# A timed pause on GpSimd in place of a limit on gathers in flight, in a kernel that sums a long convolution and a table of experts

## The chip, the cores and the metric

The kernel runs on one core of one Trainium2 chip. The metric is the device time of one execution in microseconds. Three runs of the kernel before took 960.07, 968.80 and 969.19 us; their median is 968.8 us.

## The reference

Input is `x`, 2048 rows of 448 numbers, and its row-wise layernorm `xn`. The output is `x` plus two branches that both read `xn`:

```
A: k_shift = causal depthwise convolution of k with 4 taps
   kv      = k_shift * v
   y       = causal convolution of kv with ssm_k (2048 taps, per channel, by FFT) + kv * ssm_D
   A       = xn * y
B: q       = xn @ w_q                      16 heads, two halves of 256
   s1, s2  = the halves against 64 keys each; the top 2 of each, the best 2 of the 4 sums
   e       = 64 * i1 + i2                  2 experts of 4096 per head: 32 per row
   out     = sum over the 32 of softmax(score) * gelu(xn . u[e]) * v[e]
```

Branch B reads 32 rows of `u` and 32 of `v` for each of 2048 rows, 3584 bytes a pair. That is 512 gathers of 128 pairs.

## The kernel before

Everything is float32. The 2048 rows are 16 tiles `T` of 128 partitions. `u` and `v` stand side by side in one DRAM table `uv`, so that one indexed row brings both.

*Weights* (`w_*`): `w_q` is multiplied by the keys once, which gives a matrix 448 x 2048 that maps `xn` to all scores; it is kept as a high and a low part.

*Scores* (`s_*`), tile by tile: `s_turn` transposes `xn`, `s_split` makes high and low parts, `s_mm` (L348 to L360) does the matmuls, `s_top` (L379 to L400) finds the best 8 of each 64 on VectorE (DVE) with `max` and `max_index`, and `s_gate`, `s_place` and `s_put` write for each tile the expert numbers `idx` and the gate weights `gt`.

*Experts* (`e_*`): the 32 experts of a tile's rows are laid out so that one gather brings, for 32 rows, 4 experts each onto 128 partitions. Four gathers fill one buffer `uv` (128 x 4 x 896 numbers); this document calls them a burst. There are 128 bursts and four buffers (`NBUF`). For each burst:

- `e_gather` (L490): four indirect DMAs issued by GpSimd (POOL). The first of them needs the buffer free, that is, the value matmuls of the burst four places earlier done.
- `e_dots` (L522): `xr`, the rows of `xn` spread over partitions by a matmul (`e_spread`, L503), times the gathered `u`. DVE multiplies `na` of the four in one instruction (L531), and ScalarE (ACT) sums those (`e_gelu`, L545); the other 4 - `na` DVE multiplies and sums by itself (L538). In the scores stage `na` is 4, later it is chosen by the planner's loads of the two engines.
- gelu on ACT, the gate weight on DVE (L565), and `cc`, the weights as a matmul operand, by DVE (L570) or ACT (L580).
- `e_values` (L583): the gathered `v` weighted and added on TensorE (PE), into `pv` (L593). This frees the buffer.
- after two bursts `e_out` copies `pv` (L603); after eight, `e_fold` sums on PE (L612) and DVE adds to the output rows `acc` (L614).

*Convolution* (`c_*`): the 448 channels are 112 groups of 4, and two halves `g` of 56 groups go one after the other. In each half there are an input stage (`c_load` brings `hkv` by SP in seven loads; `c_tap` and `c_prod` form `kv`; `c_in` on PE and `c_store` on ACT do the first step of the transform), a spectral stage over 33 frequencies (`c_fm` loads one matrix for each; `c_spec` L711, `c_hh`, `c_mul` with four DVE instructions L728 to L734, `c_inv` L743, `c_turn` L751), and an output stage (`c_back`, `c_zt`, `c_fin` L779, `c_gate` L788 and L793). Scores and convolution share memory, so the convolution begins behind the last score. `e_store` (L616) stores a tile's channel half by SP once that tile's experts are folded and the half's last gate is done.

*What sets the order.* The instructions of each engine run in the order in which the program emits them. That order comes from a planner (L97 to L182) that runs when the kernel is built: each operation is an `Op` with an engine, a planned cost in microseconds, and keys it waits for; the planner keeps a clock per engine, takes the operation that can start first, and settles near ties by priority. A gather has a planned cost of 1.25 on POOL, and a planned landing by its bytes. `need` (L824) makes scores urgent when they are less than `LEAD` gathers ahead of POOL's planned work. `turn` (L839) keeps the convolution in step with the gathers: it compares the share of the convolution's planned work that is done with the share of POOL's planned work since the scores' end, up to 640.0, which is 512 times 1.25. The planner sets the order only; at run time semaphores hold each instruction until its data are there.

*The limit.* `e_gather` keeps a list `sent` of all gathers and adds to each one a dependence on the gather four places earlier (L500), so a gather is issued only when that one has landed.

Of the kernel before, what the change touches and what calls it, by code (L numbers as in the profile page):

```python
# [185 lines left out]
def parallel_kernel(ctx, tc, x, wq, kk, uv, hkv, const, fq, out):  # L186
    nc = tc.nc
    ctx.enter_context(tc.manual_schedule())
    ap = ctx.enter_context(tc.tile_pool(name="ap", bufs=1))
# [8 lines left out]
    plan = Planner()  # L198
    r_sc, r_xr, r_a, r_v, r_uv = Ring(3), Ring(1), Ring(2), Ring(1), Ring(NBUF)
# [5 lines left out]
    rep = ap.tile([P, 4, 32], F32, name="rep")  # L205
    fold = rep[:, 0, :]
    half = ap.tile([P, 1], F32, name="half")
    mv = ap.tile([P, NT, 2], F32, name="mv")
    rstd = ap.tile([P, NT], F32, name="rstd")
    nmr = ap.tile([P, NT], F32, name="nmr")  # L210
    idx = ap.tile([P, NT, NG], I32, name="idx")
# [14 lines left out]
    live = {}  # L226
# [106 lines left out]
    def s_turn(tiles):  # L333

        for T in tiles:
            def turn(T=T):
                live["px", T] = ps_sc.tile([P, 512], F32, tag="sc", name="px")
                for c in range(KC + 1):
                    n = P if c < KC else KR
                    nc.tensor.matmul(live["px", T][:n, P * c:P * c + P], xn[:, T, P * c:P * c + n], ident, start=(c == 0), stop=False, skip_group_check=True)  # L340
            yield Op("PE", 0.75, turn, [("xn", T)] + ([("sc", T - 2, 3)] if T > 1 else []), key=("px", T), rings=[(r_sc, ("xl", T))], lag=0.2)
            def less(T=T):
                px, xh = live["px", T], live["xh", T][0]
                nc.tensor.matmul(px[:, :P * KC], minus, xh[:, :KC].rearrange("p c n -> p (c n)"), start=False, stop=True, skip_group_check=True)
                nc.tensor.matmul(px[:KR, P * KC:], minus[:KR, :KR], xh[:KR, KC], start=False, stop=True, skip_group_check=True)
            yield Op("PE", 0.6, less, [("xh", T)], key=("pl", T), lag=0.2)
# [138 lines left out]
    NB = len(order)  # L485
    HALF = CH * GC

    sent = []

    def e_gather():  # L490
        for b, (T, j, hf) in enumerate(order):
            for c in range(4):
                def go(b=b, T=T, g=8 * j + 4 * hf + c, c=c):
                    if c == 0:
                        live["uv", b] = gp.tile([P, 4, 2 * D], F32, tag="uv", name="uv")
                    made = nc.gpsimd.indirect_dma_start(live["uv", b][:, c, :], None, uv, bass.IndirectOffsetOnAxis(ap=idx[:, T, g:g + 1], axis=0)).ins  # L496

                    sent.append(made)
                    if len(sent) > 4:
                        tc.add_manual_dep(made, sent[-5].name, mybir.DependencyInfo(mybir.DependencyClass.Sync, mybir.DependencyReason.DATA), reason="pace")  # L500
                yield Op("POOL", 1.25, go, [("idx", T)], key=("land", b, c), moved=4.6e5, rings=[(r_uv, ("v", b))] if c == 0 else [])

    def e_spread():  # L503
        for T in range(NT):
# [299 lines left out]
    rest = range(2, NT)  # L804
# [9 lines left out]
    plan.add(2, norm(6, NT))  # L814
    plan.show("weights")
    experts = [plan.add(PRIO.get(s.__name__, 0.0), s()) for s in (e_gather, e_values, e_weigh, e_scale, e_spread, e_dots, e_gelu, e_out, e_fold)]
    stores = [plan.add(1, e_store(g)) for g in range(2)]
    plan.run(early)
# [18 lines left out]
    begun = plan.busy["POOL"]  # L837

    def turn():  # L839
        e = (plan.busy["POOL"] - begun) / (640.0 - begun)  # L840
        return -1 if plan.spent.get("conv", 0.0) / WORK < e + AHEAD else 1
    conv = []
    for g in range(2):
        for i, s in enumerate((c_load(g), c_delta(g), c_in(g, 0), c_store(g, 0), c_tap(g), c_prod(g), c_in(g, 1), c_store(g, 1),
                  c_fm(g), c_spec(g), c_hh(g), c_mul(g), c_inv(g), c_turn(g), c_back(g), c_zt(g), c_fin(g), c_gate(g))):
            conv.append(plan.add(lambda p=PRIO.get(s.__name__, 0.0): turn() + p, s, "conv"))
# [44 lines left out]
```

## Time and profile before

| | |
|---|---|
| median of three runs | 968.8 us |
| the profiled execution's own time | 975.48 us |
| its span, first to last instruction | 973.7 us |
| PE, DVE, ACT, POOL busy | 738.4, 711.1, 544.8, 492.0 us |
| mean granted clock of TensorE | 0.861 |
| moved by DMA | 278.52 MB, of it 234.91 MB by gathers |

The page lists for each engine its busy time, and for each group of instructions (line, engine, operation, what it writes and reads) how often it ran, its busy time and mean duration, the idle time of its engine just before it, and what ended that idle time. The chain is the work that ended last, followed back. DMA share is the mean busy share of the 16 DMA engines. PE rows are partly modelled, and a row on POOL is rough.

### The profile page before, as it was taken

The numbers are of one execution on the slowest core, as the hardware profiler recorded it, in microseconds if no ns is written. First come the engines' busy times: TensorE is split into PE (matmuls) and PEld (weight loads), VectorE is DVE, ScalarE is ACT, GpSimd is POOL, SyncE is SP. The second block draws the span as 40 slices with busy tenths as digits, with TensorE's granted clock in tenths as the row PEclk, the third lists the DMA queues.
The fourth block names the chain that finished last, engine by engine and source line by source line (L and its number), as shares of the span: only waits on it lengthen the run. The fifth ranks groups of instructions, "written<-read, shape, count | busy, mean of one in ns | idle before, by whom it ended". The sixth has DMA issues, their size and how long they took to land.

```text
span 973.7 us, 16544 instructions
## 1 busy us (share of the span) xinstructions
PE 738.4 (76%) x5052; PEld 421.8 (43%) x5052; DVE 711.1 (73%) x2621; ACT 544.8 (56%) x1886; POOL 492.0 (51%) x518
## 2 busy tenths in 40 slices
PE   6982989798987878846567787777777668786765
PEld 3561545455554545414344343334544424343443
DVE  3587978888787978765487788875586769788433
ACT  4325875566665665665375565554375555565532
POOL 0025562556655655555465465654545655556440
PEclk9995899898989978866677799988877898899877
DMA  9938784889888878899987699999978879999764
GB/s 344 381 125 297 248 311 152 277 280 314 292 281 275 295 263 285 271 307 377 316 284 253 219 337 330 337 310 371 319 258 264 307 266 324 327 312 338 237 219 140
DMA packets 80553, 278.52 MB, mean 286 GB/s; under 512 B 10320, under 2 KB 47568, under 8 KB 80464
## 3 DMA queue, kind: packets, MB, share of 16 engines
q0 software_dynamic: 40960, 234.91, 69.9%
q1 hardware_dynamic: 39360, 42.41, 13.0%
q8 instruction: 41, 0.67, 0.3%
q14 instruction: 48, 0.39, 0.1%
q10 hardware_dynamic: 144, 0.13, 0.1%
HBM read 273.75 MB, written 3.67 MB: 285 GB/s over the span
## 4 chain that ended last, share of the span: by engine, by line
PE 26%; DVE 23%; DMA 13%; issue 11%; ACT 9%; another core or an unknown queue 6%; POOL 5%; SPq 1%; DVEq 0%; POOLq 0%; ACTq 0%
DMA uv<-in_uv_dram,idx 11%; DVE uv L531 9%; ACT uv L550 5%; PE pv L593 5%; POOL uv L496 5%; DVE mi L397 4%; PE fin L779 3%; PE ps L683 3%; DVE mx L399 3%; DMA x<-in_hkv_dram 2%; PE sc L355 2%; PE sc L356 2%; PE sc L357 2%; PE psf L711 1%
## 5 line engine op out<-in xcount | busy, mean ns | idle before, releaser
L496 POOL DMA_INDIRECT uv<-in_uv_dram,idx x512 | 491.3, 960 | 458.4 <-issue 125.9
L550 ACT ACTIVATE uv<-uv 128x448 f32<-128x448 f32 x459 | 258.7, 567 | 80.0 <-DVE uv L531 52.5
L531 DVE TENSOR_TENSOR uv<-xr,uv 128x1792 f32<-128x1792 f32 (+3 forms) x128 | 233.2, 1823 | 38.2 <-DMA uv<-in_uv_dram,idx 21.6
L593 PE MATMUL pv<-uv,cc 128*32 128x448 f32 x1024 | 160.8, 652 | 0.2 <-ACT uv L550 0.2
L397 DVE FIND_INDEX8 mi<-mx,sc 128x8 uint32<-128x64 f32 x512 | 104.3, 221 | 7.4 <-issue 7.3
L683 PE MATMUL ps<-cst,x 128*64 128x132 f32 x896 | 82.2, 341 | 34.0 <-ACT x L693 23.3
L683 PEld LDWEIGHTS ps<-cst,x 128*64 128x64 f32 x896 | 65.6, 171 | 70.8 <-ACT x L693 38.8
L711 PE MATMUL psf<-x,fm 128*128 128x448 f32 x132 | 71.3, 630 | 30.9 <-DVE hh L734 10.1
L399 DVE MAX8 mx<-sc 128x8 f32<-128x64 f32 x512 | 73.7, 213 | 24.2 <-remote 11.5
L355 PE MATMUL sc<-wh,xh 128*128 128x512 f32 x192 | 85.3, 444 | 5.5 <-DVE mx L399 2.3
L550 ACT ACTIVATION_READ_ACCUMULATOR uv<-uv 128x1 f32 x459 | 87.2, 190 | 0.0
L356 PE MATMUL sc<-wl,xh 128*128 128x512 f32 x192 | 79.3, 413 | 0.6 <-issue 0.6
L357 PE MATMUL sc<-wh,xl 128*128 128x512 f32 x192 | 78.4, 409 | 0.3 <-issue 0.3
L743 PE MATMUL psu<-hh,fm 128*128 128x224 f32 x264 | 67.6, 386 | 9.7 <-ACT x L751 5.7
L590 PE MATMUL pv<-uv,cc 128*1 128x4 bf16 x128 | 21.6, 169 | 68.9 <-DVE cc L570 24.8
L743 PEld LDWEIGHTS psu<-hh,fm 128*128 128x128 f32 x264 | 52.7, 207 | 40.7 <-issue 27.3
L693 ACT ACTIVATE x<-ps 128x396 f32<-128x396 f32 (+1 forms) x84 | 37.2, 459 | 51.0 <-PE ps L683 34.4
L590 PEld LDWEIGHTS <-cc 128*1 128x1 bf16 x128 | 10.3, 80 | 122.3 <-issue 40.4
L565 DVE TENSOR_TENSOR w<-ge,gt 128x4 f32<-128x4 f32 x128 | 19.9, 156 | 57.1 <-ACT ge L554 41.4
L779 PE MATMUL fin<-cst,zt 128*64 128x64 f32 x896 | 46.7, 258 | 19.4 <-issue 18.8
L580 ACT ACTIVATE cc<-rep,w 128x32 f32<-128x32 f32 x212 | 50.1, 311 | 14.4 <-DVE w L565 6.1
L355 PEld LDWEIGHTS sc<-wh,xh 128*128 128x128 f32 x192 | 38.7, 201 | 42.0 <-issue 18.5
(98 smaller groups left out, 1063.0 us busy)
## 6 DMA issues: line engine op xcount, KB each, us to landing
wq<-in_wq_dram SPq DMA_DIRECT2D x16, 896.0 KB
x<-in_hkv_dram SPq DMA_DIRECT2D x14, 780.0 KB
fm<-in_fq_dram SPq DMA_DIRECT2D x66, 128.0 KB
uv<-in_uv_dram,idx POOLq DMA_INDIRECT x512
out_dram<-acc SPq DMA_DIRECT2D x32, 112.0 KB
acc<-in_x_dram SPq DMA_DIRECT2D x1, 2240.0 KB
acc<-in_x_dram SPq DMA_DIRECT2D x1, 896.0 KB
cst<-in_const_dram SPq DMA_DIRECT2D x1, 540.0 KB
```

The source lines that it names most:

```text
L355: nc.tensor.matmul(sc, xh[:, c, :], wh[:, c, ns], start=(c == 0), stop=False)
L356: nc.tensor.matmul(sc, xh[:, c, :], wl[:, c, ns], start=False, stop=False)
L357: nc.tensor.matmul(sc, xl[:, c, :], wh[:, c, ns], start=False, stop=False)
L397: nc.vector.max_index(mi[:, T % 2, 8 * n + j, :], m, sc[:, 64 * j:64 * j + 64])
L399: nc.vector.max(m, sc[:, 64 * j:64 * j + 64])
L496: made = nc.gpsimd.indirect_dma_start(live["uv", b][:, c, :], None, uv, bass.IndirectOffsetOnAxis(ap=idx[:, T, g:g + 1], axis=0)).ins
L531: nc.vector.tensor_mul(u, live["xr", T, j][:, None, :D].broadcast_to([P, na, D]), u)
L550: nc.scalar.activation(u, u, AF.Copy, accum_out=live["act", b][:, c:c + 1])
L593: nc.tensor.matmul(pv[32 * c:32 * c + 32, :D], cc[:, c, :], buf[:, c, D:], start=(hf == 0), stop=(hf == 1), tile_position=(0, 32 * c))
L683: nc.tensor.matmul(ps[64 * i:64 * i + 64, w * j:w * j + w], src, f1[:, i, :], start=True, stop=True, tile_position=(0, 64 * i))
L711: nc.tensor.matmul(ps[:, :2 * HALF], live["fm", g, q][:, 0], x1[:, :, :, q, :].rearrange("p c t k -> p t c k"), start=True, stop=True)
L743: nc.tensor.matmul(ps[:, :HALF], fm[:, 1], hh[:, i], start=(i == 0), stop=(i == 1))
```

## The change

The list `sent` and the dependence on the gather four places earlier go. Behind each fourth gather, the last of a burst, POOL runs a `memset` of 512 bytes in one partition of a new tile `idle` that nothing reads. The planner is told: the fourth gather's cost is 2.10 instead of 1.25, which makes 5.85 for a burst, and `turn` counts POOL's work up to 749.0, which is 128 times 5.85.

```diff
+    idle = ap.tile([1, 512], mybir.dt.uint8, name="idle")
...
-    sent = []
-
     def e_gather():
         for b, (T, j, hf) in enumerate(order):
             for c in range(4):
                 def go(b=b, T=T, g=8 * j + 4 * hf + c, c=c):
                     if c == 0:
                         live["uv", b] = gp.tile([P, 4, 2 * D], F32, tag="uv", name="uv")
-                    made = nc.gpsimd.indirect_dma_start(live["uv", b][:, c, :], None, uv, bass.IndirectOffsetOnAxis(ap=idx[:, T, g:g + 1], axis=0)).ins
-
-                    sent.append(made)
-                    if len(sent) > 4:
-                        tc.add_manual_dep(made, sent[-5].name, mybir.DependencyInfo(mybir.DependencyClass.Sync, mybir.DependencyReason.DATA), reason="pace")
-                yield Op("POOL", 1.25, go, [("idx", T)], key=("land", b, c), moved=4.6e5, rings=[(r_uv, ("v", b))] if c == 0 else [])
+                    nc.gpsimd.indirect_dma_start(live["uv", b][:, c, :], None, uv, bass.IndirectOffsetOnAxis(ap=idx[:, T, g:g + 1], axis=0))
+                def rest(go=go):
+                    go()
+                    nc.gpsimd.memset(idle, 0)
+                yield Op("POOL", 1.25 if c < 3 else 2.10, rest if c == 3 else go, [("idx", T)], key=("land", b, c), moved=4.6e5, rings=[(r_uv, ("v", b))] if c == 0 else [])
...
-        e = (plan.busy["POOL"] - begun) / (640.0 - begun)
+        e = (plan.busy["POOL"] - begun) / (749.0 - begun)
```

Each of the two programs has the same gathers, matmuls and transfers. What else differs follows from the plan: the order on every engine, and how many dot products go by which of the two ways (DVE alone does 62 instead of 53, ACT sums 450 instead of 459; DVE makes `cc` 80 times instead of 75).

## The prediction

> **What bounds the kernel now.** I read the page first: busy times, queues, then the costliest groups.
>
> ```profile
> span 973.7 us, 16544 instructions
> ...
> PE 738.4 (76%) x5052; PEld 421.8 (43%) x5052; DVE 711.1 (73%) x2621; ACT 544.8 (56%) x1886; POOL 492.0 (51%) x518
> ...
> q0 software_dynamic: 40960, 234.91, 69.9%
> ...
> L496 POOL DMA_INDIRECT uv<-in_uv_dram,idx x512 | 491.3, 960 | 458.4 <-issue 125.9
> ```
>
> No engine is full. The gathers' queue q0 holds the 16 DMA engines for 69.9% of the span, which is 680.6 us for 512 gathers, or 1.33 us each. POOL takes 0.96 us per gather and is otherwise idle, so something makes it wait. An average can't say what, so I cut the span by the kernel's stages: scores with experts, the two spectral stages (L711 to L751, once per channel half), and the end.
>
> ```profile
> core 0: us, PE busy (x) PEld busy (x) DVE busy (x) ACT busy (x) POOL busy (x), PEclk, DMA share, GB/s
> 162.00:426.00 264.00, 221.85 (x1206) 131.61 (x1204) 217.85 (x1250) 165.59 (x630) 154.75 (x164) 0.91 0.85 283
> 545.00:651.00 106.00, 84.15 (x392) 41.26 (x384) 91.28 (x188) 62.92 (x219) 64.00 (x68) 0.95 0.92 324
> 794.00:897.00 103.00, 78.87 (x360) 39.33 (x360) 86.90 (x175) 59.01 (x204) 60.88 (x65) 0.92 0.93 325
> 897.00:974.00 77.00, 49.13 (x617) 32.12 (x617) 33.82 (x68) 29.30 (x87) 26.07 (x28) 0.82 0.60 205
> ```
>
> In the scores window PE (84%) and DVE (83%) are both nearly full. In the spectral windows DVE stands at 86% and 84% and the DMA share at 0.92 and 0.93. Next, POOL's gathers in the scores window (first row), the first spectral window (second and third) and the second one (fourth), with what ended its idle time, and its two longest waits at the end (last two).
>
> ```profile
> L496 POOL DMA_INDIRECT uv<-in_uv_dram,idx x164 | 155.0, 945 | 122.0 <-issue 42.5 <-PE pv L593 26.4 <-DVE mi L397 24.5
> L496 POOL DMA_INDIRECT uv<-in_uv_dram,idx x68 | 64.2, 945 | 49.3 <-issue 20.0 <-DMA uv<-in_uv_dram,idx 9.6 <-ACT vs L603 9.3
> POOL uv L496 <- ACT vs L603: 9.3, 1, 9.3
> L496 POOL DMA_INDIRECT uv<-in_uv_dram,idx x65 | 61.4, 945 | 42.1 <-issue 16.2 <-DMA uv<-in_uv_dram,idx 13.8 <-ACT uv L550 3.7
> ...
> POOL uv L496 <- PE pv L593: 8.1, 1, 8.1
> POOL uv L496 <- PE pf L612: 6.7, 1, 6.7
> ```
>
> In the scores stage and at the end POOL waits for engines: a gather's buffer is still being read. In the spectral windows the named releaser is the issue gap or an earlier gather: there the limit of four sets the pace. The timeline shows the shape of one burst (four gathers into one buffer).
>
> ```profile
> 213.04 0.94 POOL L496 DMA_INDIRECT uv<-in_uv_dram,idx  x1 [1.36 <-PE pv L593]
> 214.29 0.94 POOL L496 DMA_INDIRECT uv<-in_uv_dram,idx  x1 [0.30 <-issue]
> 215.53 0.95 POOL L496 DMA_INDIRECT uv<-in_uv_dram,idx  x1 [0.30 <-issue]
> 216.78 0.95 POOL L496 DMA_INDIRECT uv<-in_uv_dram,idx  x1 [0.30 <-issue]
> 219.09 0.94 POOL L496 DMA_INDIRECT uv<-in_uv_dram,idx  x1 [1.36 <-PE px L345]
> ```
>
> Gathers leave 1.25 us apart, 0.30 of it the issue gap, and before the next burst stands a gap of 1.36 us: 6.05 us per burst where nothing else holds it. The fifth gather waits for the landing of the first.
>
> **The change, part by part.** First, *the limit goes*. In the spectral windows POOL's idle time beyond the issue gaps was 49.3 - 9.3 - 67 x 0.30 = 19.9 us in 17 bursts, 1.17 us each, and 42.1 - 65 x 0.30 = 22.6 us in 16.25 bursts, 1.39 each. The limit isn't gone altogether: in the changed program's instruction order the first eight gathers carry no wait for an earlier one, and from the ninth on each still waits for the gather eight places earlier (the completion semaphores go round in eight). Eight gathers take at least 10 us to issue; landings on the chain take 5 to 8.3 us, so I cost this wait at nothing.
>
> ```profile
> 607.10 5.02 DMA uv<-in_uv_dram,idx
> ...
> 708.88 8.34 DMA uv<-in_uv_dram,idx
> ```
>
> Second, *the pause*: 128 memsets of 512 bytes on one partition. No such instruction is in the trace; the nearest are POOL's memsets of 1 and of 128 elements per partition.
>
> ```profile
> L880 POOL MEMSET const-float32-0.0<- 128x1 f32 x1 | 0.1, 98 | 0.2 <-issue 0.2
> masks.py:197 POOL MEMSET ident<- 128x128 f32 x1 | 0.2, 204 | 0.3 <-POOLq L880 0.3
> ```
>
> 106 ns for 127 more elements is 0.83 ns each, so 512 elements take 0.098 + 511 x 0.00083 = 0.52 us, and with one more issue gap of 0.30 the pause is 0.82 us (an estimate from these rows). Below it could be the shortest memset alone, 0.10; above, a whole gather's slot, 1.25. Behind the memset on POOL only the next burst is queued; where that waits for a buffer the pause hides in the wait. A free burst then takes 5.00 + 0.82 = 5.82 us.
>
> What pace alone could give in the spectral windows is 17 x (1.17 - 0.82) + 16.25 x (1.39 - 0.82) = 6.0 + 9.3 = 15 us; with a pause of 0.10 it is 39, with 1.25 about 1. But late next is DVE. It takes the gathered rows at L531, and only its idle time ahead of that line can go:
>
> ```profile
> L531 DVE TENSOR_TENSOR uv<-xr,uv 128x1792 f32<-128x1792 f32 (+1 forms) x17 | 32.5, 1909 | 5.4 <-issue 3.0 <-DMA uv<-in_uv_dram,idx 2.2
> L531 DVE TENSOR_TENSOR uv<-xr,uv 128x1792 f32<-128x1792 f32 (+1 forms) x17 | 32.9, 1938 | 9.1 <-DMA uv<-in_uv_dram,idx 5.7 <-PE pv L593 2.3 <-issue 1.0
> ```
>
> That is 5.4 and, without the PE part, 6.7 us: 12 us, which I take (0 to 31, since DVE idles 30.8 us in the two windows in all). Elsewhere gathers run ahead of the engines, and pace is worth nothing.
>
> Third, *the plan*. POOL's planned cost of a burst grows from 5.00 to 5.85, so all five instruction streams are ordered anew. By PE's order, in bursts whose value matmuls (L593) stand ahead: the last score matmul 49 before, 44 after; the stretch of PE's work for each stage 55-65, 65-82, 83-90 and 90-100, 100-119, 120-126 before; 50-61, 61-77, 78-85 and 84-96, 97-113, 114-122 after. So the scores stage loses 5 bursts, input and output stages gain 5 in sum, the spectral stages lose 4, and 6 bursts instead of 2 stand behind the convolution. A burst's own work on DVE, in the first spectral window:
>
> ```profile
> L570 DVE TENSOR_TENSOR cc<-rep,w 128x128 f32<-128x128 f32 x17 | 5.0, 292 | 0.8
> L565 DVE TENSOR_TENSOR w<-ge,gt 128x4 f32<-128x4 f32 x17 | 2.7, 156 | 0.9 <-ACT uv L550 0.7
> L538 DVE SCALAR_TENSOR_TENSOR uv<-xr,uv 128x448 f32<-128x448 f32 x4 | 2.5, 618 | 0.0
> ```
>
> With L531 that is 42.7 / 17 = 2.5 us, a burst's price where engines are full; where gathers set the pace it is 5.82. Scores: between 2.5 and 264/41 = 6.4; of POOL's waits beyond the issue gap there (122.0 - 164 x 0.30 = 72.8) 26.4 + 24.5 = 50.9 end on PE and DVE, 70%, so 0.7 x 2.5 + 0.3 x 6.4 = 3.7, and 5 bursts are -18 us. Input and output stages: +5 x 2.5 = +12. Spectral, with DVE the bound by now: -4 x 2.5 = -10. Behind the convolution: +4 x 5.82 = +23. The output stage that ends the convolution spreads over 8 bursts instead of 6, which should take a quarter of POOL's 14.8 us of waits there, -4. DVE's split of the dot products changes little (nine single-row products more, nine ACT sums less) and is inside these prices.
>
> Fourth, *the stores*. The second channel half can be stored only behind the last gate, so 17 stores leave in a row at the end:
>
> ```profile
> 962.98 8.28 SPq L619 DMA_DIRECT2D out_dram<-acc  x17
> 966.33 0.62 DVE L614 TENSOR_TENSOR acc<-pf,acc 128x448 f32<-128x448 f32 x1 [2.66 <-PE pf L612]
> ```
>
> The last sum is done at 966.95, but the last store's issue ends only at 971.26. With 6 bursts behind the convolution the others are out before: -4.
>
> The sum: -12 - 18 + 12 - 10 + 23 - 4 - 4 = -13 us, so the profiled execution would have a span of 961. Its own time was 975.48 us, 0.7% over the median of the runs, 968.8 (960.07 to 969.19). Taken off that median: 956 us.
>
> **Rivals.** *Engines keep the time.* POOL waits less but DVE's own chain fills the gaps; pace is worth 0 instead of 12 us. For it: DVE at 84 to 86%, and only 7.9 us of its idle time in the two spectral windows is put down to gathers by name. The sum is -1: 968 us.
>
> *The bursts behind the convolution* (slower). Six bursts with nothing beside them cost 23 us more, and what left the scores stage doesn't pay: at DVE's price it gives 5 x 2.5 = 12 there, while in the input and output stages, where conv work and bursts alternate on PE, each of the 5 more costs 4 us (20). Then -12 + 20 - 10 + 23 - 4 = +17: 986 us. It decides once the bursts taken out of the scores stage shorten it by under 3 us each. Against it: the tail costs it nothing that the stage 897-974, with its two long waits, didn't pay before.
>
> *Loads stand behind gathers* (slower). With eight on their way in place of four, a load of `hkv` could wait for four more gathers, 4 x 1.33 = 5.3 us. DVE waits for these loads six times:
>
> ```profile
> DVE x L666 <- DMA x<-in_hkv_dram: 18.3, 6, 5.6
> 450.00:475.00 25.00, 15.18 (x142) 9.78 (x138) 10.24 (x28) 11.36 (x38) 13.06 (x14) 0.77 1.05 373
> ```
>
> That would be 32 us: 988 us. Against it: in that window both kinds run at once at 373 GB/s, and the gathers were slowed (14 in 25 us), not the loads alone. [...]
>
> *The pause is dear* (slower). It decides above 1.9 us: from the first gather's start to the last's are 950.0 - 65.4 = 884.6 us over 511 steps, 6.92 per burst, less 5.00. At 2.5 us the gathers alone need 65.4 + 127 x 7.5 + 24 = 1042 us.
>
> ```profile
> L496 POOL DMA_INDIRECT uv<-in_uv_dram,idx x512: 940/946/1464, 65.4 to 950.0; - x171
> ```
>
> *Gathers paced everything* (much faster): scores bursts at 6.4 (-32) and the whole of DVE's idle time (-31) instead of -18 and -12 give -46: 923 us.
>
> **How the numbers follow.** Forecast 0.42, with a range of its own of 938 to 965; engines keep the time 0.20; bursts behind the convolution 0.24; loads 0.06; pause 0.03; gathers paced everything 0.05. The time is the forecast's, 956. About 1% (959 to 978) is what a measurement here can tell from no change. Three quarters of the forecast's weight (0.31), a quarter of the first rival's (0.05) and the last rival (0.05) lie below: faster 0.41. Same: 0.11 + 0.10 = 0.21. Slower: 0.24 + 0.06 + 0.03 + 0.05 = 0.38. The range leaves out the last rival, the dear pause and a little beyond the slow ones: 930 to 988.
>
> **What will show it.** The memset's row should read 0.4 to 0.6 us and free bursts 5.6 to 5.9 us apart; above 6.9 the pause is the bound. In the spectral stages DVE should stand at 90% or more with L531's idle time nearly gone; if it stays at 85%, the first rival holds. The scores stage should end some 18 us earlier, and fewer than 17 stores should stand in a row at the end, with four more bursts behind the convolution. Waits for `hkv` above 18.3 us would mean the loads. I am wrong if the new order itself makes engines wait for one another anywhere; that can't be priced from this trace.

## The result and the profile after

The changed kernel took 1006.8 us (four runs, 1001.37 to 1009.19) where the kernel before took 969.0: a ratio of 1.0395, 95% interval 1.0328 to 1.0462. Forecast was 956, with a range of 930 to 988. The profiled execution took 1006.68 us. Medians here are of all runs, but the ratios leave out slow runs, those more than 1.5% above the fastest of the same kernel (two runs of the kernel before in the last set, 1049 and 1226 us, among them). The page of the changed kernel:

```profile
span 1004.9 us, 16699 instructions
...
PE 734.6 (73%) x5052; PEld 410.0 (41%) x5052; DVE 710.5 (71%) x2644; ACT 537.0 (53%) x1848; POOL 560.1 (56%) x646
...
q0 software_dynamic: 40960, 234.91, 68.3%
...
DVE 33%; PE 26%; ACT 14%; issue 10%; another core or an unknown queue 8%; DMA 8%; SPq 1%; POOL 1%; DVEq 0%; ACTq 0%; POOLq 0%
```

PE, DVE and ACT are no busier than before (DVE 711.1, now 710.5 us), and of POOL's 68 us more the fills are 65.9, so the 31 us that the span has grown are waits. The last line is the chain that ended last. The same four stretches as in the prediction, moved to where the stages now lie (scores with experts, the two spectral stages, the end behind the convolution):

```profile
162.00:421.00 259.00, 210.13 (x1169) 124.87 (x1167) 211.47 (x1258) 156.31 (x589) 165.92 (x193) 0.95 0.81 271
542.00:642.00 100.00, 77.92 (x361) 39.29 (x357) 87.27 (x180) 57.18 (x199) 64.77 (x76) 0.95 0.90 312
797.00:899.00 102.00, 77.38 (x338) 37.67 (x338) 81.72 (x171) 53.38 (x187) 62.25 (x73) 0.92 0.85 297
971.00:1005.00 34.00, 14.52 (x78) 2.65 (x74) 14.80 (x30) 13.07 (x45) 12.37 (x15) 0.55 0.62 221
```

No engine and no transfer has become much fuller: DMA stands at 0.90 and 0.85 in the spectral stages (0.92 and 0.93 before), DVE at 87% and 80% (86% and 84%). And yet the gathers no longer keep DVE waiting there. Its wide product in the two stretches:

```profile
L529 DVE TENSOR_TENSOR uv<-xr,uv 128x1792 f32<-128x1792 f32 (+1 forms) x16 | 30.9, 1932 | 0.1
```
```profile
L529 DVE TENSOR_TENSOR uv<-xr,uv 128x1792 f32<-128x1792 f32 (+1 forms) x14 | 26.8, 1915 | 1.9 <-DMA uv<-in_uv_dram,idx 1.9
```

The idle time ahead of that line was 5.4 and 9.1 us. What has grown instead are waits whose end the profile can't name. In the chain above they are 8%; in the chain of before they were 6%:

```profile
PE 26%; DVE 23%; DMA 13%; issue 11%; ACT 9%; another core or an unknown queue 6%; POOL 5%; SPq 1%; DVEq 0%; POOLq 0%; ACTq 0%
```

In the list of waits (us in total, times, longest) they read "remote". First before, then after:

```profile
ACT zt L766 <- remote: 44.4, 11, 6.4
...
ACT idx L461 <- remote: 29.7, 5, 7.0
...
DVE fin L788 <- remote: 17.4, 5, 5.7
```
```profile
ACT zt L764 <- remote: 41.1, 10, 8.0
...
DVE fin L786 <- remote: 34.3, 7, 7.4
...
ACT idx L462 <- remote: 25.6, 4, 11.9
ACT x L691 <- remote: 23.9, 12, 5.1
...
DVE x L664 <- DMA x<-in_hkv_dram: 8.9, 1, 8.9
```

All such waits together are 144 us in 46 waits before and 207 us in 57 after. This program runs on one core and waits for no other, so "remote" can't be taken by its word. The last row is DVE's wait for `hkv`, which fell from 18.3 us.

### The profile page after: what moved, and what is told of

The parts are those of the page before. It is cut to its first block, busy times and chain, and to the rows that moved or that the text cites. A ratio compares the mean times of both kernels' runs of the same rounds, so it can differ in the third digit from the quotient of the medians.

```text
span 1004.9 us, 16699 instructions
## 1 busy us (share of the span) xinstructions
PE 734.6 (73%) x5052; PEld 410.0 (41%) x5052; DVE 710.5 (71%) x2644; ACT 537.0 (53%) x1848; POOL 560.1 (56%) x646
## 3 DMA queue, kind: packets, MB, share of 16 engines
q0 software_dynamic: 40960, 234.91, 68.3%
## 4 chain that ended last, share of the span: by engine, by line
DVE 33%; PE 26%; ACT 14%; issue 10%; another core or an unknown queue 8%; DMA 8%; SPq 1%; POOL 1%; DVEq 0%; ACTq 0%; POOLq 0%
DVE uv L529 11%; ACT uv L548 8%; DVE mi L398 8%; PE pv L591 5%; DVE mx L400 5%; PE ps L681 3%; DMA uv<-in_uv_dram,idx 3%; PE fin L777 3%; PE psf L709 2%; DMA x<-in_hkv_dram 2%; DMA wq<-in_wq_dram 2%; PE xr L510 2%; PE pw L297 2%; PE psu L741 2%
## 5 line engine op out<-in xcount | busy, mean ns | idle before, releaser
L548 ACT ACTIVATE uv<-uv 128x448 f32<-128x448 f32 x450 | 253.5, 567 | 70.1 <-DVE uv L529 39.8
L529 DVE TENSOR_TENSOR uv<-xr,uv 128x1792 f32<-128x1792 f32 (+3 forms) x128 | 228.8, 1790 | 20.0 <-remote 13.3
L591 PE MATMUL pv<-uv,cc 128*32 128x448 f32 x1024 | 169.7, 657 | 2.8 <-issue 2.8
L681 PE MATMUL ps<-cst,x 128*64 128x132 f32 x896 | 75.1, 318 | 50.1 <-issue 33.3
L681 PEld LDWEIGHTS ps<-cst,x 128*64 128x64 f32 x896 | 57.9, 156 | 85.8 <-issue 50.7
L356 PE MATMUL sc<-wh,xh 128*128 128x512 f32 x192 | 82.9, 432 | 4.4 <-remote 1.9
L588 PE MATMUL pv<-uv,cc 128*1 128x4 bf16 x128 | 21.6, 168 | 82.9 <-ACT cc L578 44.4
L741 PE MATMUL psu<-hh,fm 128*128 128x224 f32 x264 | 68.3, 386 | 15.0 <-DVE acc L612 4.1
L357 PE MATMUL sc<-wl,xh 128*128 128x512 f32 x192 | 77.2, 402 | 0.1
L498 POOL MEMSET idle<- 1x512 uint8 x128 | 65.9, 515 | 0.0
L578 ACT ACTIVATE cc<-rep,w 128x32 f32<-128x32 f32 x192 | 45.9, 313 | 34.5 <-DVE w L563 19.5
```

Source lines behind the costliest of these rows:

```text
L356: nc.tensor.matmul(sc, xh[:, c, :], wh[:, c, ns], start=(c == 0), stop=False)
L357: nc.tensor.matmul(sc, xh[:, c, :], wl[:, c, ns], start=False, stop=False)
L529: nc.vector.tensor_mul(u, live["xr", T, j][:, None, :D].broadcast_to([P, na, D]), u)
L548: nc.scalar.activation(u, u, AF.Copy, accum_out=live["act", b][:, c:c + 1])
L591: nc.tensor.matmul(pv[32 * c:32 * c + 32, :D], cc[:, c, :], buf[:, c, D:], start=(hf == 0), stop=(hf == 1), tile_position=(0, 32 * c))
L681: nc.tensor.matmul(ps[64 * i:64 * i + 64, w * j:w * j + w], src, f1[:, i, :], start=True, stop=True, tile_position=(0, 64 * i))
```

## The experiments

**First set: limit, pause and plan apart.** All four ran on one chip; the kernel before took 968.1 us there. Theory one: the new order makes the engines wait for one another. Theory two: the order is harmless or good, and the loss comes with the missing limit.

*The plan alone* (`a_plan_only`): the limit of four stays and there is no fill. The order on PE, DVE, ACT and SP is that of the changed kernel.

```diff
-                yield Op("POOL", 1.25, go, [("idx", T)], ...
+                yield Op("POOL", 1.25 if c < 3 else 2.10, go, [("idx", T)], ...
...
-        e = (plan.busy["POOL"] - begun) / (640.0 - begun)
+        e = (plan.busy["POOL"] - begun) / (749.0 - begun)
```

> The kernel before, limit of four kept and no memset, but with the changed plan (2.10 for a fourth gather, 749.0): PE, DVE, ACT and SP get exactly the changed kernel's order. Theory one, the order: the convolution ends at about 970 us whatever is between, and the bursts left behind it come on top, so nearly all of the 38 us is here: 990 to 1012 us. Theory two, the pace (pause and deeper queue cost the time): 960 to 975 us, as before.

Measured: 954.75 us, ratio 0.9868 (0.9767 to 0.9970).

*Fill without limit, old plan* (`b_pause_only`): the changed kernel with the planned costs of before.

```diff
-                yield Op("POOL", 1.25 if c < 3 else 2.10, rest if c == 3 else go, ...
+                yield Op("POOL", 1.25, rest if c == 3 else go, ...
...
-        e = (plan.busy["POOL"] - begun) / (749.0 - begun)
+        e = (plan.busy["POOL"] - begun) / (640.0 - begun)
```

> The changed kernel, memset and no limit of four, but with the plan of before (1.25, 640.0): PE, DVE, ACT and SP get exactly the order of before. Theory one, the order: 945 to 972 us, a little less than before where gathers set the pace in the spectral stages. Theory two, the pace: 995 to 1010 us, as the changed kernel.

Measured: 1003.93 us, 1.0390 (1.0312 to 1.0467).

*No limit, no fill, old plan* (`c_free`): as the last, and the fill goes too.

```diff
                 def rest(go=go):
                     go()
-                    nc.gpsimd.memset(idle, 0)
```

> Plan of before, neither the limit of four nor the memset: only the wait for the gather eight places earlier is left. Theory one, the order: 945 to 972 us, within 1% of the run with the pause alone, since gathers run ahead of the engines in most stages. Theory two, the pace: if the deeper queue is what costs, 995 us or more; if the memset is, below the run with the pause alone by over 20 us.

Measured: 1005.10 us, 1.0426 (1.0339 to 1.0513).

*No limit, and a plan that believes in faster gathers* (`v4_fast_plan`; the edit is shown against `c_free`): 56 bursts instead of 49 ahead of the last score matmul.

```diff
-    HOP, SLIP, RATE = 0.20, 1.20, 0.35
+    HOP, SLIP, RATE = 0.20, 1.20, 0.42
...
-                yield Op("POOL", 1.25, rest if c == 3 else go, ...
+                yield Op("POOL", 1.15, rest if c == 3 else go, ...
...
-        e = (plan.busy["POOL"] - begun) / (640.0 - begun)
+        e = (plan.busy["POOL"] - begun) / (588.8 - begun)
```

> As the kernel with neither limit nor memset, but planned with faster gathers (1.15 on POOL, a planned rate of 0.42 in place of 0.35, the convolution's measure 588.8): 56 bursts stand ahead of the last score matmul on PE in place of 49, the convolution ends behind 125 in place of 126. Theory one, the order, in its strong form (a burst in the scores stage costs next to nothing): last score matmul still at 405 to 425 us, the convolution's last gate earlier than 955 us, 935 to 965 us in all. Theory one in its weak form (only bursts behind the convolution count): 955 to 975. Theory two: as the run with neither.

Measured: 1022.68 us, 1.0586 (1.0479 to 1.0694).

Theory one falls: the very order that I had feared gains 1.3% where the limit stays, and the old order loses 4.3% where it goes. The fill changes nothing that can be measured (1.0390 against 1.0426, the intervals overlap). The loss comes with the missing limit. The fast plan lost 17.6 us more than `c_free`, which neither theory had said: an order can cost something too, though not the order of the changed kernel. How does the missing limit cost time? `c_free` differs from the kernel before only in what POOL waits for, and the busy times are the same (DVE 710.3 us, PE 738.5). The first step of its delay lies at 76 us. DVE's timeline there (start, duration, idle time before it and what ended that):

```profile
76.67 0.19 DVE L419 TENSOR_TENSOR best<-mx 128x32 f32<-128x32 f32 x1 [0.23 <-issue]
77.37 0.20 DVE L420 TENSOR_TENSOR other<-mx 128x16 f32<-128x16 f32 x1 [0.51 <-issue]
80.23 0.18 DVE L421 TENSOR_TENSOR dd<-best,other 128x16 f32<-128x16 f32 x1 [2.67 <-remote]
...
83.05 0.17 DVE L445 TENSOR_TENSOR e<-e,sl 128x16 f32<-128x16 f32 x1 [1.23 <-DVE e L444]
...
85.89 0.18 DVE L251 BATCH_NORM_AGGREGATE mv<-st 128x2 f32<-128x6 f32 x1 [1.84 <-remote]
```

These are short DVE instructions that need only the DVE instruction before them, and still one of them starts 2.67 us after that has ended. The packed trace also keeps moments at which semaphores were raised. DVE's own was raised, by these records, at 80.21, 83.03 and 85.87, and the starts at 80.23, 83.05 and 85.89 stand 0.02 us behind. So in these three places DVE starts at once when its semaphore is up, and it is the semaphore that comes late: L420 had ended at 77.57. The same happens between engines. DVE's last index operation ended at 179.61; the matmul that waits for it, on a PE that was done at 180.57, started at 183.00. DVE's next instruction needs, by the program's own counts, only the matmul that ended at 178.07 (first row; PE's ends are modelled). DVE was free at 179.61 and started at 188.71, 9.1 us late:

```profile
177.68 0.39 PE L360 MATMUL sc<-wr,xl 128*128 128x512 f32 x1
...
179.37 0.24 DVE L398 FIND_INDEX8 mi<-mx,sc 128x8 uint32<-128x64 f32 x1 [0.49 <-issue]
...
180.18 0.39 PE L360 MATMUL sc<-wr,xl 128*128 128x512 f32 x1
183.00 0.74 PE L356 MATMUL sc<-wh,xh 128*128 128x512 f32 x1 [2.44 <-remote]
183.54 0.63 PE L357 MATMUL sc<-wl,xh 128*128 128x512 f32 x1
...
188.71 1.15 DVE L400 MAX8 mx<-sc 128x8 f32<-128x64 f32 x8 [9.10 <-PE sc L360]
```

I call these late starts. Behind PE's, at 183.00, its work was slower too: a matmul took 0.63 us where it had taken 0.39, while the granted clock stood at 0.50 for 3.41 us (the columns are the stretch, its length, PE busy, granted clock, DMA share and GB/s):

```profile
180.60:183.09 2.49, 0.09 (x1) 1.00 1.00 386
183.09:186.50 3.41, 3.41 (x8) 0.50 1.01 408
186.50:189.90 3.40, 0.88 (x4) 1.00 0.84 316
```

PE had been idle for 2.44 us when the clock fell, and the clock was back at 1.00 after 3.41 us of work. That the pause brought it down is how I read this one place; no run tests it.

To count them I took, for each instruction on PE, DVE and ACT that waits for no DMA, the moment at which the last thing it waits for was done (the instruction before it on its engine, or the one that raises its semaphore by the program's own counts), and called a start more than 0.5 us behind that late:

| kernel | time, us | late starts | their sum, us |
|---|---|---|---|
| before | 975.5 | 107 | 203 |
| plan alone | 953.9 | 89 | 176 |
| fill, no limit | 1004 | 109 | 259 |
| no limit | 1001.2 | 114 | 259 |
| changed kernel | 1006.7 | 113 | 262 |

They are hardly more in number but longer; 225 of the 259 us without a limit are instructions of ACT and DVE that wait for PE. Nearly all of those that wait for a semaphore stand less than 0.1 us behind a recorded raise of it (89 of 93 before, 93 of 97 with no limit). They stand where gathers pile up. Share of the time, by how many gathers were on their way, in which at least one late start was pending (a gather counts from the end of its issue to the last of its 80 packets; five were on their way for under 10 us):

| on their way | 1 | 2 | 3 | 4 |
|---|---|---|---|---|
| before | 0.01 | 0.18 | 0.28 | 0.41 |
| no limit | 0.03 | 0.15 | 0.43 | 0.60 |
| changed kernel | 0.05 | 0.19 | 0.41 | 0.50 |

**Second set: how deep, how close.** Theory one: each further gather on its way makes late starts worse. Theory two: what costs is that POOL issues without ever being stopped. For the limit of three there is a third: four was only just enough.

*Limits of three and six* (`limit3`, `limit6`), for three:

```diff
-                    if len(sent) > 4:
-                        tc.add_manual_dep(made, sent[-5].name, ...
+                    if len(sent) > 3:
+                        tc.add_manual_dep(made, sent[-4].name, ...
```

> The kernel before with a limit of three gathers on their way in place of four; nothing else changes and the order on every engine is that of before. Theory one (depth: each further gather on its way makes the other engines start their ready instructions later): the late starts fall below those of before, while a free burst grows, since the fourth gather now waits for the landing of the first; 955 to 985 us. Theory two (what costs is that GpSimd issues without ever being stopped, whatever lies in the queue): 955 to 985 as well, so this run does not part them; it shows whether four is the best limit. Theory three (four was only just enough, the gathers' pace is what the engines wait for): over 1000.

> The kernel before with a limit of six gathers on their way in place of four; the order on every engine is that of before. Theory one (depth): the time lies between that with four (968) and that without the limit (1005), 975 to 1000, since up to five and six gathers are on their way at once. Theory two (GpSimd never stopped): with six the wait hardly ever stops it, so 1000 to 1010, as without the limit. If neither holds and the limit's exact place doesn't matter, 962 to 972.

*A short fill behind every gather* (`pause_each`), on `c_free`:

```diff
+                    nc.gpsimd.memset(idle[:, :1], 0)
                 def rest(go=go):
```

> The kernel before without the limit of four, and behind every gather a fill of one byte on GpSimd (about 0.1 us and an issue gap of 0.30), so that a gather leaves every 1.65 us instead of every 1.25, slower than the 1.33 us for which a gather holds the DMA engines; order as before. Theory one (depth): the queue can't build up, so the late starts go: 950 to 985, the upper part because a free burst now takes 6.6 us where it took 6.05. Theory two (GpSimd is never stopped and issues or fills without a break): 1000 us or more, as without the limit. If the free bursts' pace were what counts, 985 to 1000.

*The changed kernel with the limit put back* (`after_with_limit`):

```diff
-                    nc.gpsimd.indirect_dma_start(live["uv", b][:, c, :], ...
+                    made = nc.gpsimd.indirect_dma_start(live["uv", b][:, c, :], ...
+                    sent.append(made)
+                    if len(sent) > 4:
+                        tc.add_manual_dep(made, sent[-5].name, ...
```

> The changed kernel with the limit of four put back: the fill behind each fourth gather stays, the plan stays. Both theories: the whole loss of the change lies in the missing limit, so this is at most the plan alone (954.8) plus what the fill costs; a free burst grows from 6.05 us by nothing where the wait for a landing covers the fill, and by 0.8 us where it doesn't: 953 to 972. Against both, if the fill itself harms: over 980.

Measured: this set fell on another chip, and there the kernel before itself took 896.9 us. Limit of three: 1039.73 us, ratio 1.1610 (1.1546 to 1.1674). Limit of six: 841.35, 0.9415 (0.9357 to 0.9473). A fill behind each gather: 846.92, 0.9459 (0.9403 to 0.9514). The changed kernel with its limit: 898.84, 1.0016 (0.9986 to 1.0047). Theories one and two had no time under 950 and the sign of the limit wrong for this chip; only the third, that four was only just enough, came out. And the fill behind each gather didn't do what it was meant to. It took 0.09 us and vanished in the issue gap, so gathers left 1.25 us apart (the median step), as without it, and not 1.65:

```profile
472.27 0.95 POOL L495 DMA_INDIRECT uv<-in_uv_dram,idx  x1 [0.21 <-issue]
473.21 0.09 POOL L496 MEMSET idle<- 1x1 uint8 x1
473.52 0.94 POOL L495 DMA_INDIRECT uv<-in_uv_dram,idx  x1 [0.21 <-issue]
```

What differs between the two chips shows in the chain that ended last, of the changed kernel with its limit:

```profile
DMA 34%; DVE 32%; PE 11%; POOL 9%; issue 7%; ACT 4%; SPq 3%; DVEq 0%; POOLq 0%; ACTq 0%
```

There is no share for another core or an unknown queue, and the list of waits has not one "remote". The count of late starts, 89 to 114 in the traces above, is 1 here in each of the four (1.3 us). It isn't the DMA that is less busy here: the gathers' queue stands at 74.9% (68.3% in the changed kernel's first trace) and at 76.7% with a limit of six. Nor is it TensorE's clock, which with a limit of three was 0.842 on average, lower than in any kernel above, with one late start. But one more thing differs. The packed traces of the late kind lack about half of the records of semaphore raises: 8140 in the kernel before and 7827 with no limit, against 14397 here with a limit of six, in the same order on PE, DVE, ACT and SP. The records of instructions (16544, 16542 and 16542) and of DMA packets (80564, 80566 and 80566) are all there.

**Third set: both kinds of chip.** Theory one: there are two kinds of chip, one with late starts (late chips) and one without (prompt chips); on the first kind gathers crowded together make them worse, on the second the limit only holds the gathers back. Theory two: a limit is needed everywhere, and six is a better one. The kernels are unaltered copies.

> The changed kernel once more, unaltered, because the kernel before took 968 us on the chip of the first runs and 897 on the chip of the second. Theory one (two conditions: in the first one ready instructions start late, at moments that the profile puts down to something unknown, and the more so without the limit; in the second these late starts don't exist, and there the limit of four is what holds the gathers back): where the kernel before takes about 897 us, this takes 835 to 865; where it takes about 968, this takes 1000 to 1010 again. Theory two (a limit is needed everywhere, and six is merely a better one than four): 900 us or more even where the kernel before takes 897.

> The kernel before without the limit and without the fill, once more. Theory one: 830 to 850 us where the kernel before takes about 897, 1000 to 1010 where it takes 968. Theory two (a limit is needed everywhere): 900 or more in both.

> The kernel before with a limit of six, once more. Theory one: 835 to 850 us where the kernel before takes about 897; 975 to 1005 where it takes 968, since more gathers on their way bring more late starts there. Theory two (six is the better limit everywhere): 890 to 930 where the kernel before takes 968.

> The kernel before, unaltered, for a trace of it from the same chip as the three others. Theory one: where it takes about 897 us, the chain that ended last has no share for another core or an unknown queue (6% in the first trace), DVE's and ACT's waits named remote nearly vanish, and the chain's DMA share is 30% or more; where it takes 968, the chain is like that of the first trace. Theory two (the two chips differ in the speed of DMA or of the engines): the unknown share stays at 4% or more, and a gather's landing or a matmul's duration differs by 5% or more from the first trace.

Measured: a third chip, of the late kind; the kernel before took 952.4 us. Changed kernel: 973.95 (960.60 to 983.52), which is 1.023 as a ratio of medians, without an interval; its two lower runs alone would give 1.015. No limit: 994.83, 1.0425 (1.0344 to 1.0506). Limit of six: 997.89, 1.0451 (1.0400 to 1.0503). The copy of before: 0.9988 (0.9945 to 1.0031). The unknown share is back in the chain, 4% in the copy of before and 6% to 8% without the limit of four, and so are the late starts (without that limit 98 to 110, 217 to 246 us). Theory two falls: six, the best limit on the prompt chip, is as bad here as none. The changed kernel lost less than on the first chip, below what I expected of it, and no limit came out a little below its 1000 to 1010 too.

**Fourth set: the change on a prompt chip.** Left open was whether late starts come with gathers close behind each other (theory one) or with busy DMA engines as such (theory two), and what the change does where there are none.

> No limit, and a fill of one byte behind every gather, so that gathers leave 1.65 us apart, slower than the 1.33 us for which one holds the DMA engines. Theory one (the late starts come with gathers that stand close behind each other): where the kernel before takes 950 us or more, the late starts stay at the level of the kernel before and the time is 940 to 975. Theory two (they come with the DMA engines being busy at all, however the gathers are spaced): 985 to 1005, as without the limit. Where the kernel before takes about 897 there are no late starts, and both say 840 to 852.

> A limit of three. Theory one: where the kernel before takes 950 us or more, the late starts fall to less than half of those of the kernel before, but the gathers alone need some 1030 us, so 1035 to 1050. Theory two: the late starts stay and come on top of the gathers' pace: 1055 to 1090. Where the kernel before takes about 897 both say 1035 to 1045.

> The changed kernel, unaltered. Where the kernel before takes 950 us or more: 965 to 1010 (both theories; it has no limit and leaves bursts of four close together). Where the kernel before takes about 897: 835 to 865, because there the limit is what holds the gathers back; if a limit is needed there too, 897 or more.

> The kernel before without the limit. Where the kernel before takes 950 us or more: 985 to 1010 (both theories). Where it takes about 897: 828 to 848, at most the time with a limit of six (841).

Measured: a chip of the prompt kind, the kernel before at 898.0 us. The changed kernel: 854.96 us, ratio 0.9522 (0.9437 to 0.9606). No limit: 844.47, 0.9408 (0.9371 to 0.9445). Fill behind each gather: 844.54, 0.9410 (0.9362 to 0.9459). Limit of three: 1040.49, 1.1579 (1.1496 to 1.1662). Here the change is 4.8% faster. The first steps of the first set's stretch show what is missing, in `c_free` on this chip:

```profile
73.63 0.18 DVE L420 TENSOR_TENSOR other<-mx 128x16 f32<-128x16 f32 x1
73.85 0.17 DVE L421 TENSOR_TENSOR dd<-best,other 128x16 f32<-128x16 f32 x1
...
74.78 0.17 DVE L445 TENSOR_TENSOR e<-e,sl 128x16 f32<-128x16 f32 x1
...
75.81 0.18 DVE L251 BATCH_NORM_AGGREGATE mv<-st 128x2 f32<-128x6 f32 x1
```

The work from L420 to L251, 8.5 us apart on the late chip, is 2.2 us apart here. With that gone, POOL's gathers and DVE's wide product are what the limit touches. Their groups (busy and mean, then idle time before them), in the changed kernel with its limit of four:

```profile
L497 POOL DMA_INDIRECT uv<-in_uv_dram,idx x512 | 493.5, 964 | 321.3 <-DMA uv<-in_uv_dram,idx 92.0
...
L535 DVE TENSOR_TENSOR uv<-xr,uv 128x1792 f32<-128x1792 f32 (+3 forms) x128 | 229.5, 1794 | 83.4 <-DMA uv<-in_uv_dram,idx 82.4
```

and without it, in the changed kernel itself:

```profile
L495 POOL DMA_INDIRECT uv<-in_uv_dram,idx x512 | 495.7, 968 | 268.5 <-issue 117.8
...
L529 DVE TENSOR_TENSOR uv<-xr,uv 128x1792 f32<-128x1792 f32 (+3 forms) x128 | 229.4, 1793 | 26.4 <-DMA uv<-in_uv_dram,idx 21.6
```

DVE's wait for gathered rows falls from 82.4 to 21.6 us, and the span with it from 897.1 to 846.7 (two prompt chips, on which the kernel before took 896.9 and 898.0). Little of that stands where the prediction had looked for it: in the two spectral stages DVE's wait falls from 15.1 to 6.0 us, but between them, with the output stage of the first half and the input stage of the second, from 28.9 to 1.7. There, with the limit and then without:

```profile
L535 DVE TENSOR_TENSOR uv<-xr,uv 128x1344 f32<-128x1344 f32 (+3 forms) x20 | 30.2, 1510 | 29.0 <-DMA uv<-in_uv_dram,idx 28.9
```
```profile
L529 DVE TENSOR_TENSOR uv<-xr,uv 128x1344 f32<-128x1344 f32 (+3 forms) x20 | 30.1, 1505 | 3.9 <-PE xr L510 2.3 <-DMA uv<-in_uv_dram,idx 1.7
```

With a limit of three, POOL's wait for landings is 230.2 us and the gathers are 58% of the chain.

**Last set.** The question of spacing was put once more.

> No limit, and a fill of one byte behind every gather (a gather every 1.65 us). Where the kernel before takes 940 us or more: theory one (late starts come with gathers close behind each other) 940 to 975, theory two (they come with busy DMA engines as such, however the gathers are spaced) 985 to 1005. Where it takes about 897, both say 840 to 852, as measured there.

> A limit of three. Where the kernel before takes 940 us or more: theory one 1035 to 1050 with late starts under half of those of the kernel before, theory two 1055 to 1090 with as many. Where it takes about 897: 1035 to 1045, as measured there.

It fell on the prompt chip of the fourth set again: the kernel before 896.6 us; 842.97, ratio 0.9418 (0.9348 to 0.9489), and 1041.34, ratio 1.1584 (1.1484 to 1.1684). Both repeat what was known there, and neither speaks of the late kind. Nor could this fill have parted the two theories on a late chip, since it doesn't set the gathers further apart.

## Why the prediction was wrong, point by point

*The limit goes* (-12 us). This is the step that failed. What it named did happen: in the spectral stages of the changed kernel the idle time ahead of DVE's wide product fell by 12.5 us, as the prices had it. The one wait that it costed at nothing, for the gather eight places earlier, was rightly so: in the first trace of the changed kernel at most five gathers were on their way at once, and five for 0.8 us. But the sum has no term for anything else that answers to more gathers on their way. In the first set the same edit alone cost 37 us by the medians (4.3% by the ratio) where the term has -12. With them come late starts that are 56 us longer in sum, part of them beside other work; the limit of four had been holding them down. On a prompt chip the same edit gains 5.9%, 54 us, which is more than the 31 us that I allowed at most for this term. So the term was wrong in sign on the one kind and too small on the other. Too small it was because of the sentence that elsewhere pace is worth nothing: on the prompt chips most of the wait for gathers that went stood outside the spectral stages. Even the page of before puts 21.6 us of that idle time down to gathers, where the two spectral windows have 7.9, so 13.7 stood elsewhere already.

*The sign for the first rival.* DVE stood at 87% and 80% in the spectral stages, and not at the 90% or more of the forecast. By the sign that I had named this means that engines keep the time. But L531's idle time did go; over the whole span waits named "remote" grew from 144 to 207 us.

*What I had read past.* The page of before showed 6% of the chain, some 54 us, under another core or an unknown queue, and 144 us of waits named remote. None of the rivals gave that time a cause, so none could ask whether the change would make it grow. The names of releasers in that trace are incomplete besides, with about half of the semaphore records lacking, and the prices rest on these names. The sentence on what would make the forecast wrong named the new order, and the plan alone showed that the order was not it.

*The pause.* The memset took 515 ns against an estimated 0.52 us. The full issue gap that I added to it didn't come: the fill starts at once behind the gather and only 0.16 us stand behind it. Free bursts are 5.37 us apart, here on the fourth set's chip, instead of 5.82, which is outside the 5.6 to 5.9 that I had named:

```profile
L498 POOL MEMSET idle<- 1x512 uint8 x128 | 65.9, 515 | 0.0
```
```profile
459.42 0.95 POOL L495 DMA_INDIRECT uv<-in_uv_dram,idx  x1 [0.16 <-PE psu L741]
...
464.12 0.51 POOL L498 MEMSET idle<- 1x512 uint8 x1
464.79 0.95 POOL L495 DMA_INDIRECT uv<-in_uv_dram,idx  x1 [0.16 <-issue]
```

The first row is of the changed kernel's first trace, the others of its trace from the fourth set. On a late chip the pause cost nothing that could be measured. On a prompt one it was not run apart from the plan; 512 fills of one byte cost nothing there (0.9410 against 0.9408), since they fit into the issue gap.

*The plan* (-18 + 12 - 10 + 23 - 4 - 4 = -1 us). With the limit kept it measured -13 us on a late chip (interval -2.3% to -0.3%) and, with the fill, nothing on a prompt one (1.0016). On the late chip its last score matmul came at 386 us where the kernel before had it at 414 on a chip of the same kind: 28 us earlier for 18 predicted. From their first matmul to their last (L711 and L743), its spectral stages took 99.1 and 100.7 us for 109.9 and 115.7: 26 us less for 10 predicted. In the changed kernel the last score matmul came at 410 only, which I put down to the late starts, so the four more bursts behind the convolution were not paid for. These are the weight loads of the last score matmul, plan alone and then the changed kernel:

```profile
L359 PEld LDWEIGHTS sc<-wr,xl x64: 187/188/330, 33.7 to 385.6; 128*128 128x128 f32 x64
```
```profile
L360 PEld LDWEIGHTS sc<-wr,xl x64: 187/188/334, 34.0 to 409.7; 128*128 128x128 f32 x64
```

*The tail and the stores* (+23, -4). From the start of the last gate's sum (973.33 us) to that of the last fold's (1001.01) it took 27.7 us for six bursts; before, with two, that was 962.3 to 966.3. +23 was the right size. The end behind the last fold's sum shrank from 6.8 to 3.3 us, as the stores' term had it.

*The rivals.* Slower had a chance of 0.38 and came out on the first chip, but for none of the three causes that I had priced, so that share of the chances was right by luck. *Bursts behind the convolution:* their 23 us were right, but the scores stage did pay when the limit stayed. The sum of this rival also leaves out the pace (-12) and one of the two -4 without saying so; with them it is +1, about 970. *Loads behind gathers:* on the first chip DVE's wait for `hkv` fell from 18.3 to 8.9 us, where this rival had 32 us more. Why it fell, no run shows. On the prompt chips those waits did grow, from 14.8 us with the limit to 26.2 on DVE and 11.5 on ACT without. The engines also ask for the loads earlier there, and no run parts the two. *The pause is dear:* it added 0.37 us to a burst, far from 1.9. *Gathers paced everything:* its 923 us are 0.953 of the median, and a prompt chip measured 0.9522. That the ratios agree is chance. DVE's waits for gathers were the reason, but the rival had its gain in the scores and spectral stages, and most of it came between and behind them.

*What stays open.* Nearly every late start that waits for a semaphore (89 of 93 before, 93 of 97 with no limit) is a semaphore that comes late, up to 10.3 us behind the instruction that raises it (in the changed kernel of the third set). What holds it up, no run shows. It is not a longer instruction (DVE's wide product took 1823 ns in the kernel before and 1822 on a prompt chip with a limit of six, ACT's sum 567 and 566), not a fuller DMA queue (68.3% in the changed kernel, 74.9% on a prompt chip with its limit), not TensorE's clock (0.842 with one late start), and not the order (the kernel before took 968.1 us on one chip and 896.9 on another). The late traces also lack about half of their semaphore records (8140 against 14397), but no run shows whether the one has to do with the other. Whether the chip itself or something else on it makes it late or prompt is not shown either: two chips that could be told apart were late, two were prompt, and the second prompt one was so twice. The link between gathers on their way and late starts rests on the limit (four against six and none) and on the table of shares. That it is their number, and not that POOL is hardly ever stopped, is not shown: six and none cost the same on the late chip of the third set (997.89 and 994.83 us), which fits both. Whether spacing the gathers would do as well on a late chip was not measured: all three runs with a fill behind every gather fell on prompt ones, and that fill doesn't space them.

No version beat both kernels everywhere. On a late chip the best is the plan with the limit kept (954.75 against 968.1 and 1006.8). On a prompt chip it is no limit, or one of six, with the old plan (841 to 847 us against 897 and 855); there the new plan and its fill together cost some 10 us (854.96 against 844.47, and the intervals of the two ratios just touch).

## What to carry to other kernels

Time in the chain that no engine and no transfer owns ("remote", an unknown queue) is a term of the sum like any other: before taking a limit away, ask whether that time could be what the limit holds down. A limit on transfers in flight is worth measuring at several depths and on more than one chip: four here was 6% too tight on one kind of chip and 4% better than none on the other. Count the semaphore records of a trace before trusting the names of releasers in it: in the late ones half were lacking. When a change combines an edit and a new plan, run each alone first; here they had opposite signs. And look whether a pause moves what it is to space: a fill of 0.09 us vanished in a gap of 0.30.

## What the hardware did that I had not expected

The same program took 952 to 969 us on some chips and 897 on others, with nearly the same busy time on DVE (711.1 and, with a limit of six, 703.8 us) and the same bytes. On a late chip even DVE instructions that depend only on DVE started late, by 2.67 us in `c_free` and by up to 3.45 in the changed kernel, though nearly all late starts that wait for a semaphore stood less than 0.1 us behind its recorded raise (89 of 93 before, 93 of 97 in `c_free`). A limit of three gathers in flight instead of four cost 16% on a prompt chip, one of six gained 6%, and beyond six nothing was left to gain (0.9415 against 0.9408 with none).
